# All of x0 as fp32 over hardware queues, part of the softmax on GpSimd, four exp transposes on TensorE, and a new order table in a fused attention and expert kernel

## The chip, the cores and the metric

The kernel runs on one core of a Trainium2 chip. A core has TensorE (PE, matrix products and transposes into PSUM), VectorE (DVE), ScalarE (ACT), GpSimd (POOL), SyncE (SP, which here only issues DMAs) and 16 DMA engines that all queues share. DMAs issued by SP and ACT go through hardware queues, those of POOL through a software queue, and only the latter convert a type on the way. The metric is the device time of one execution in microseconds, lower is better.

## The reference, cut to what matters

```python
B, H, S, Ns, D = (8, 8, 512, 32, 64)           # x: [B,H,S,D], state: [B,H,Ns,D], all fp32
scores  = softmax(scale * x @ state.T)         # over the 32 states   ("A side")
xread   = scores @ state                       # [B,H,512,64]
scores2 = softmax(scale * state @ x.T)         # over the 512 tokens  ("B side")
sread   = scores2 @ x                          # [B,H,32,64]
t = concat([xread, sread], axis=2) -> [N=4352, 512]
P = exp(t @ w_gate - max)                      # [N, 8]
for _ in range(8):                             # Sinkhorn
    P /= P.sum(1) + 1e-9;  P /= P.sum(0) + 1e-9;  P *= N / 8
out = sum over e of P[:, e] * (relu(t @ w1[e]) @ w2[e])    # w1 [8,512,1024], w2 [8,1024,512]
```

## The kernel before

All products run in fp16. The first part, up to some 134 us, is issued from a table (`PLAN`): every operation is made as an `Op` in program order and gets a number, and `issue` (L105) emits them in the order of the table. "63P" means operation 63 on PE; V is DVE, A is ACT, G is POOL, S is SP's DMA queue, H is bookkeeping of the program alone. Each engine runs its operations in that order and waits in it. The pairs of numbers at each `Op` (costs in us), ranks and due times served to make the table; nothing of them is computed on the chip. After the table, experts 1 to 7 run in plain loops (`layer1`, `layer2`, L263 to L387).

What the table holds, with the lines:

- **State.** Two DMAs of 256 KB (L441, SP and ACT) bring it as fp32; two copies each (L483) place it twice side by side as fp16; sixteen PE transposes (L492) and four evictions (L496) make stT, the state transposed. stD (L504 to L512) is a block form of it for the first two units.
- **x.** For each of the 8 batches two DMAs on POOL's queue (L468) bring x converted to fp16 into x_nat, which has four buffers, so that the load of batch 4 waits for the last reader of batch 0. Batches 0 and 1 are transposed by PE (L578) and evicted (L582), the others by transposing DMAs on SP (L591). The result is xT.
- **Units.** Half a batch (four heads) is a unit, u = 2b + q, 16 in all. A score product (L605) fills psB, of which there is one buffer: the next unit's score waits until this one's is read. A side: DVE turns the scores (L628, "flip"), takes maxima (L631), subtracts (L648), ACT takes exp (L656), DVE sums and takes reciprocals (L666, L667), DVE or POOL normalizes (L670), DVE turns back into aT (L674). Units 0 and 1 instead have a score product straight in token order (L684, then L688 and L691), and a transpose back by PE (L709) with an eviction (L712). B side: maximum (L640), bias (L644), exp with sum on ACT (L652), reciprocal (L659), normalization on DVE or POOL (L662), a transposing DMA on SP (L742) into ETs, a product with x (L758, "read") and an eviction into xsT.
- **Expert 0.** V = stT x w1 (L870), a hidden product of 512 tokens in eight blocks from V and aT (L897), relu on ACT or DVE (L425, L427), output product in halves (L935) and its eviction into acc (L419, L421). acc is first written here.
- **Gates and Sinkhorn.** Gate products (L788), the global maximum (L814 to L825), then eight rounds of row normalization (L829 to L833), a column sum by PE (L846) and column normalization (L839 to L841).
- **Towards expert 1.** Its weights, two V products, the hidden blocks of batch 0, and eight differences of weight halves, T (L965), all on DVE.

Weights come in four DMAs per expert on POOL's queue (L545, L548). An operation that writes PSUM or a buffer takes a slot of a ring and waits until the slot's last users are done.

Of the kernel before, what the change touches and what calls it, by code (L numbers as in the profile page):

```python
# [16 lines left out]
6G 0S 1S 2V 7H 44V 3A 33V 32A 34A 8G 56P 36P 35V 55H 37V 10H 45V 57A 42P 58V 9G 38P 40P 43A 59P 4S 39A 41V 5V  # L17
46V 62P 50H 51G 61A 71V 63P 60A 52G 64V 11G 72V 73A 80P 65V 12G 435P 401P 66A 81V 13H 79P 14G 82V 436A 88V
437A 404P 83A 67V 402A 137H 403A 89V 96H 97P 100P 84V 406A 68V 90A 98A 15G 85V 69P 86P 53G 405A 99V 87V 70A
103P 101A 102A 91V 409P 16H 92G 413P 104V 407P 410A 411P 105V 111A 438P 120P 414V 408A 419P 421P 106V 415P  # L20
112V 138S 121V 74V 439A 412A 422V 113V 417P 107A 54G 440A 75G 122V 432P 429P 123V 370V 420A 469P 128A 418A
416A 17G 108V 140P 124A 125V 423P 426P 471A 433P 114A 148V 93S 129V 430P 149V 172H 424P 76S 434A 115V 470A
109G 130V 139S 110V 126G 141V 131A 427P 18G 127V 142V 428V 431A 445P 143V 132V 94P 150A 95V 77P 425A 156P 116G
447P 151V 133V 78V 449P 446A 443P 441P 144A 455P 164V 152G 448A 117S 19H 450V 157V 444A 165V 173S 442A 451P
456A 166A 134S 20G 452A 453P 463P 158V 472P 207H 145V 175P 159V 183V 184V 457P 31G 146G 454A 176V 473A 160A
464P 185A 174S 460P 458P 461P 465A 147V 161V 21G 153S 177V 191P 47P 162G 474A 118P 167V 459A 154P 462A 178V
163V 135P 49A 168G 199V 22H 48V 179A 466P 136A 352P 475P 200V 192V 201A 193V 119V 467P 476A 194V 23G 195A 485P
202V 208S 210P 180V 169S 155A 218V 356P 353A 481P 357V 468A 487P 219V 24G 489P 181G 186V 211V 242H 486A 482A
477P 490V 488A 483P 479P 220A 170P 478A 503P 187G 480A 484V 171A 203G 196V 537P 209S 25H 212V 226P 197G 504A
505A 506P 213V 500P 182V 198V 26G 234V 221V 507A 222V 204S 188S 491P 27G 538A 227V 539A 501P 497P 502A 508A  # L30
492P 235V 243S 228V 244S 214A 229V 511P 215V 236A 523P 230A 498P 494P 216G 245P 495P 515P 512V 499A 277H 231V
524A 493A 517P 246V 253V 223S 496A 247V 521P 516A 237V 254V 519P 509P 522V 518A 248V 513P 232G 189P 520A 255A
205P 510V 224P 514V 540P 28H 278S 261P 249A 190V 269V 29G 225A 270V 262V 531P 534P 206V 238G 250V 532P 256V
358P 271A 535P 217V 541A 533A 233V 542A 312H 279S 263V 272V 536A 354P 280P 528P 543P 529P 525P 288V 289V 251G
555P 264V 281V 265A 282V 239S 257V 526P 359A 266V 544A 530V 556A 545P 355A 547P 549P 273G 553P 527A 546V 571P
313S 290A 548A 283V 605P 550A 554V 296P 267G 606V 304V 572A 305V 240P 573A 557P 284A 607A 558A 551P 297V 552A
568P 360P 258S 241V 285V 30G 291V 306A 559P 562P 574P 298V 252V 315P 299V 286V 569P 576A 268V 323V 563P 575A
274S 300A 560P 570A 292G 316V 361A 561A 581P 564A 307V 565P 362P 324V 317V 301V 325A 302G 566P 363V 582A 326V
579P 587P 583P 287V 314S 588V 591P 567A 580A 639P 608P 584A 592A 347H 303V 331P 577P 348G 641V 640A 610A 609A
339V 293S 589P 585P 275P 332V 259P 578A 327G 586A 260A 590A 294P 340V 308G 333V 341A 593P 309S 318V 319A 334V  # L40
295V 364P 594P 276V 328S 625P 619P 342V 595A 335A 365A 599P 320V 602P 343V 336V 600P 337V 603P 626A 321G 322V
329P 310P 350G 344S 601A 349G 311A 620V 345P 338V 346V 604V 366P 596P 330A 368P 369V 351G 597P 367A 371V 611P
372P 598A 695H 615P 617P 373V 612V 374P 375V 613P 614V 616A 623P 618A 621P 696H 711H 376A 705P 377V 642P 624A
622A 706A 707A 630P 643V 697V 708P 644A 378P 379V 631P 710A 627P 698V 380V 647P 632A 709A 636P 628P 381P 633P
699V 648V 637P 382V 634P 657P 629A 638A 383V 700V 653P 658A 655P 384P 651P 635A 701V 654A 725P 385V 723P 386V
702V 656A 726A 716P 652A 724A 717A 645P 659P 649P 714P 646A 650A 660A 387P 721P 715A 712P 727P 687P 722A 388V
728A 688A 667P 713A 664P 389V 390P 703V 665P 668P 391V 673P 674A 392V 661P 670P 669A 729V 393P 671P 394V 666A
662P 672A 677P 395V 718P 663A 678A 679P 675P 683P 719A 681P 720V 680A 676A 685P 396P 684A 682A 397V 686A 692P
704V 689P 693P 690P 730P 398V 694A 399P 733P 731V 691A 732A 735A 734A 400V
""".split()  # L50
ENGINES = {"P": "PE", "V": "DVE", "A": "ACT", "G": "POOL", "D": "DMA", "S": "SPQ", "H": "HOST"}
NT_ = 2
ETX = 0
POOLB = 1
# [50 lines left out]
def issue(ops):  # L105
    for step in PLAN:
        op = ops[int(step[:-1])]
        assert all(d.end for d in op.after) and ENGINES[step[-1]] in op.on
        for slot in op.takes:
            slot.ring.taken.append(slot)  # L110
            slot.tile = slot.make()
        op.emit(ENGINES[step[-1]])
        op.end = True
    assert all(op.end for op in ops) and len(PLAN) == len(ops)
# [3 lines left out]
def kernel(  # L118
# [99 lines left out]
    etp = actx.enter_context(tc.tile_pool(name="attn_et", bufs=3))  # L218
# [216 lines left out]
    st_in = spl.tile([128, B, NQ, 2, D], FP16, name="st_in")  # L435
    st_st = spl.tile([128, B, NQ, D], FP32, name="st_st")
    loads = []
    for g in range(2):
        def load(g=g):
            bs = ds(g * B // 2, B // 2)  # L440
            (nc.scalar if g else nc.sync).dma_start(  # L441
                out=st_st[:, bs], in_=state[bs].rearrange("b (q h) n d -> (h n) b q d", q=NQ))

        loads.append(dma((0, 0), 1.0, load, lands=2.7))
        ops[-1].since, ops[-1].hard = 0.5, 1
# [5 lines left out]
    wgd = dma((0, 2), 0.1, lambda: nc.sync.dma_start(  # L451
        out=wg_st, in_=moe_w_gate.rearrange("(kc p) e -> p kc e", p=128)))
    wgc = op((15.0,), {"DVE": (0.15, 0.25)}, lambda _: nc.vector.tensor_copy(out=wgh, in_=wg_st), [wgd])
    wgc.since = 20.0
# [7 lines left out]
    for b in range(B):  # L462
        x_ready.append([])
        part("x%d" % b)
        got = op((0, 1 + 2 * b), {"HOST": (0.0, 0.0)}, lambda _: None, takes=[xn[b]])
        for g in range(2):
            def load(b=b, g=g):
                nc.gpsimd.dma_start(  # L468
                    out=xn[b].tile[:, ds(g * 4, 4), :],
                    in_=x[b, ds(g * 4, 4), :, :].rearrange("h (p sc) d -> p h (sc d)", sc=NSC))  # L470

            x_ready[b].append(dma((0, 1 + 2 * b, g), 1.28 if b else 2.3 - 0.6 * g, load, [got], [], [xn[b]], "POOL"))
            ops[-1].since, ops[-1].hard = 0.7, 1
# [4 lines left out]
    bd = []  # L478
    for g in range(2):
        for s_ in range(2):  # L480
            def place(eng, g=g, s_=s_):
                bs = ds(g * B // 2, B // 2)
                copy(eng, st_in[:, bs, :, s_, :], st_st[:, bs])  # L483

            bd.append(op((0, 0, g), {"DVE": (0.50, 0.64)} if s_ else {"ACT": (0.50, 0.65)}, place, loads[g:g + 1] + warmed))
    stT_ready = []
    for g in range(4):
        ps = psum([128, 4, 128], FP16, "stT_ps")

        def turn(_, g=g, ps=ps):  # L490
            for i in range(4):
                nc.tensor.transpose(ps.tile[:, i], st_in[:, 2 * g + i // 2, i % 2].rearrange("p s d -> p (s d)"),  # L492
                                    identh)

        def keep(eng, g=g, ps=ps):
            copy(eng, stT[:, ds(2 * g, 2)].rearrange("p b q c -> p (b q) c"), ps.tile)  # L496

        t = op((0, 1, g), {"PE": (0.35, 0.55)}, turn, bd[g // 2 * 2:g // 2 * 2 + 2] + [makeh], [ps])
        stT_ready.append(op((0, 1, g), EVICT16, keep, [t], uses=[ps]))
    ND = (TOK + 1) // 2  # L500
    stD_ready = {}
    if TOK:
        stD = spl.tile([128, ND, NQ, 4, 2, Ns], FP16, name="stD")
        zd = op((0, 0, 0), {"POOL": (0.40, 0.50), "DVE": (0.25, 0.35)}, lambda eng: engines[eng].memset(stD, 0.0))  # L504
        for b in range(ND):
            def spread(eng, s_, b=b):
# [4 lines left out]
                               lambda eng, s_=s_, spread=spread: spread(eng, s_), stT_ready[b // 2:b // 2 + 1] + [zd])  # L511
# [55 lines left out]
    for b in range(B):  # L567
# [4 lines left out]
                  [x_ready[b][0]], [xT])  # L572
        for g in range(2 if b < NT else 0):
# [11 lines left out]
            t = op((due_x(2 * b + g) - 2.0, 0), {"PE": (0.70, 0.88)}, turnX, [x_ready[b][g], makeh], [ps], [xn[b]])  # L585
# [3 lines left out]
        for g in range(0 if b < NT else 2):  # L589
# [5 lines left out]
            xt_ready.append([dma((due_x(2 * b - 2), 0, g), 2.0, turn, [x_ready[b][g], gotT], [], [xn[b], xT], lands=0.8)])  # L595
            ops[-1].moves, ops[-1].xbar = (3.0, 0.8), 1
            ops[-1].on = {"SPQ": (1.4, 4.5)}
        for q in range(NQ):
# [18 lines left out]
            o2 = op((due_x(2 * b + q), 0), {"PE": (0.13, 0.38)}, score, xt_ready[q] + stT_ready,  # L617
# [5 lines left out]
            E2 = slot(etp, 3, [128, S], FP16, "E2")  # L623
            a16 = slot(asb, 2, [128, S // 32, Ns], FP16, "a16")
            ETs = slot(etp, 3, [128, NSC, 128], FP16, "ETs")
# [402 lines left out]
    n = 0  # L1028
# [79 lines left out]
```

## Time and profile before

| what | us |
|---|---|
| median of 3 runs (753.98 to 754.52) | 754.13 |
| the profiled execution, device time | 753.05 |
| its span, first to last instruction | 751.3 |
| first transpose of x on PE (L578) | 6.98 |
| first hidden product of expert 0 (L897) | 18.66 |
| first row normalization of Sinkhorn (L829) | 102.90 |
| last product of the table before expert 1's A (L334) | 134.45 |
| DVE busy in 20 to 100 us | 73.2 of 80 |

When the loads of the first 25 us were issued and how long they took shows in the DMA issues of the first 40 us: x_nat 5.9 us to landing in the median, w1h 8.7, w2h 10.4, the two state loads 4.9 and 4.3, the transposing DMAs 5.0 and 4.8. The profile lists busy time per engine, then waits with the one who ended them; the clock column of a stretch is the share of full speed that TensorE was granted.

### The profile page before, as it was taken

What the parts mean: (1) busy time and instruction counts of PE and PEld (TensorE: products, weight loads), DVE (VectorE), ACT (ScalarE), POOL (GpSimd) and SP (SyncE); (2) the same over time, 40 slices, a digit from 0 to 9 for tenths busy, and PEclk for the clock granted to TensorE, in tenths of its full rate; (3) what the DMA queues carried; (4) which work ended last, traced back from release to release, by engine and by line L of the source; (5) the groups of instructions that cost most, each with busy time, mean ns of one, the idle gap of its engine ahead of it and who ended that gap; (6) DMA issues with size and microseconds to landing.
All of it is one profiled execution on the core that took longest, in us unless ns stands there. A gap on an engine that the chain in (4) does not pass through costs nothing.

```text
span 751.3 us, 16144 instructions
## 1 busy us (share of the span) xinstructions
PE 734.7 (98%) x6517; PEld 501.2 (67%) x6517; DVE 616.3 (82%) x1529; ACT 518.2 (69%) x1014; POOL 70.8 (9%) x81
## 2 busy tenths in 40 slices
PE   4999999999999999999999999999999999999997
PEld 3444445667677777777777677776777777776776
DVE  5999989888888789788887888887897888878875
ACT  6876846798976766666666766667667666676662
POOL 3664310200010000100000000100001000000000
PEclk9999999999999999999999999999999999999999
DMA  9997560600032000600006000330006000002234
GB/s 175 151 133 127 86 92 1 113 2 1 1 66 48 2 1 2 113 1 1 2 4 110 2 1 1 58 56 1 1 2 112 2 1 2 1 29 101 98 113 141
DMA packets 51323, 36.71 MB, mean 49 GB/s; under 512 B 25392, under 2 KB 43824, under 8 KB 51248
## 3 DMA queue, kind: packets, MB, share of 16 engines
q0 software_dynamic: 22272, 20.97, 18.4%
q1 hardware_dynamic: 27744, 14.18, 7.7%
q8 instruction: 51, 0.84, 0.5%
q10 hardware_dynamic: 1232, 0.52, 0.3%
q14 instruction: 24, 0.20, 0.1%
HBM read 42.48 MB, written 8.91 MB: 68 GB/s over the span
## 4 chain that ended last, share of the span: by engine, by line
PE 91%; DVE 3%; DMA 2%; ACT 1%; POOL 1%; issue 0%; SPq 0%; POOLq 0%; ACTq 0%
PE hps L255 28%; PE Bseed L334 20%; PE A L334 14%; PE E L334 13%; PE yps L935 6%; PE v_ps L235 4%; PE hps L897 4%; DMA xT<-x_nat 2%; DMA x_nat<-in_x_dram 1%; DVE acc L348 1%; ACT Hm L275 1%; PE su_ps L758 0%; PE y L312 0%; PE v_ps L870 0%; POOL E L662 0%; ACT V L419 0%
## 5 line engine op out<-in xcount | busy, mean ns | idle before, releaser
L275 ACT ACTIVATE Hm<-hps 128x512 f16<-128x512 f32 (+1 forms) x496 | 265.2, 577 | 128.1 <-PE hps L255 125.3
L255 PE MATMUL hps<-aT,V 128*128 128x512 f16 x880 | 230.1, 379 | 0.0
L334 PEld LDWEIGHTS <-Hm 128*128 128x128 f16 x1888 | 181.4, 98 | 71.2 <-issue 15.8
L348 DVE SCALAR_TENSOR_TENSOR acc<-Bseed,Pmat,acc 128x256 f32<-128x256 f32 x354 | 155.0, 477 | 9.4 <-PE Bseed L334 6.6
L334 PEld LDWEIGHTS <-sm 128*128 128x128 f16 x1416 | 138.2, 98 | 34.1 <-issue 0.4
L334 PE MATMUL A<-w2h,Hm 128*128 128x256 f16 x944 | 123.7, 273 | 0.0
L334 PE MATMUL Bseed<-T,Hm 128*128 128x256 f16 x944 | 123.3, 273 | 0.0
L255 PEld LDWEIGHTS <-V 128*128 128x128 f16 x880 | 86.1, 98 | 51.3
L348 DVE SCALAR_TENSOR_TENSOR acc<-E,Pmat,acc 128x256 f32<-128x256 f32 x236 | 103.1, 476 | 12.5 <-PE E L334 12.5
L281 DVE TENSOR_TENSOR sm<-Hm 128x512 f16<-128x512 f16 (+1 forms) x122 | 50.1, 411 | 64.2 <-ACT Hm L275 64.0
L243 ACT CAST V<-v_ps 128x512 f16<-128x512 f32 x150 | 77.7, 611 | 0.0
L348 DVE SCALAR_TENSOR_TENSOR acc<-A,Pmat,acc 128x256 f32<-128x256 f32 x118 | 51.9, 479 | 17.2 <-PE A L334 16.7
L935 PE MATMUL yps<-w2h,hT 128*128 128x512 f16 x272 | 64.1, 379 | 0.0
L363 ACT COPY Bseed<-A 128x512 f32<-128x512 f32 (+1 forms) x62 | 34.1, 550 | 43.3 <-PE A L334 42.1
L334 PE MATMUL E<-T,sm 128*128 128x256 f16 x472 | 61.7, 273 | 0.0
L334 PE MATMUL E<-w2h,sm 128*128 128x256 f16 x472 | 61.7, 273 | 0.0
L334 PE MATMUL Bseed<-T,sm 128*128 128x256 f16 x472 | 61.5, 272 | 0.0
L282 DVE TENSOR_TENSOR Hm<-Hm 128x512 f16<-128x512 f16 (+1 forms) x122 | 50.2, 412 | 4.2
L284 DVE TENSOR_TENSOR sm<-Hm,sm 128x512 f16<-128x512 f16 (+1 forms) x122 | 50.2, 412 | 4.2
L283 DVE TENSOR_TENSOR sm<-sm,Hm 128x512 f16<-128x512 f16 (+1 forms) x122 | 49.4, 405 | 0.0
L194 POOL DMA_DIRECT2D w1h<-in_moe_w_dram x12 | 8.5, 714 | 397.9 <-PE hps L255 397.4
L935 PEld LDWEIGHTS <-hT 128*128 128x128 f16 x272 | 25.4, 99 | 28.8 <-issue 1.7
(127 smaller groups left out, 609.7 us busy)
## 6 DMA issues: line engine op xcount, KB each, us to landing
w1h<-in_moe_w_dram POOLq DMA_DIRECT2D x16, 512.0 KB, 7.0
w2h<-in_moe_w_dram POOLq DMA_DIRECT2D x16, 512.0 KB, 8.1
out_dram<-acc SPq DMA_DIRECT2D x32, 256.0 KB, 2.6
x_nat<-in_x_dram POOLq DMA_DIRECT2D x16, 256.0 KB, 5.6
st_st<-in_state_dram ACTq DMA_DIRECT2D x1, 256.0 KB, 4.9
st_st<-in_state_dram SPq DMA_DIRECT2D x1, 256.0 KB, 4.3
ETs<-E SPq DMA_TRANSPOSE x16, 3.9
out_dram<-acc SPq DMA_DIRECT2D x4, 64.0 KB, 1.7
```

The lines of the kernel that those rows point to most:

```text
L235: nc.tensor.matmul(ps[q][ds(j * Ns, Ns), :], stT[ds(r, 64), bi, q, ds((j ^ q) * Ns, Ns)], w1h[ds(r, 64), 2 * q + j // 2, cols], tile_posit ...
L243: nc.scalar.copy(out=dst, in_=src)
L255: nc.tensor.matmul(out, lhs, rhs, start=(k == 0), stop=(k == len(terms) - 1))
L275: nc.scalar.activation(out=Hm[:, i, j, :tn], in_=hps[:, :tn], func=AF.Relu)
L281: nc.vector.tensor_add(s1, a21, a22)
L282: nc.vector.tensor_sub(a21, a11, a21)
L283: nc.vector.tensor_sub(s2, s1, a11)
L284: nc.vector.tensor_sub(s4, a12, s2)
L334: nc.tensor.matmul(dst[:, c], lhs(j, c), rhs[:, j], start=first and c == 0 and j == 0, stop=(j == NJ - 1), skip_group_check=True)
L348: nc.vector.scalar_tensor_tensor(out=dst, in0=src[:, c], scalar=p[:, k], in1=dst, op0=ALU.mult, op1=ALU.add)
L363: nc.scalar.copy(out=Bb[:, :nk], in_=A[:, :nk])
L935: nc.tensor.matmul(yps.tile, hT[fb].tile[:, ds(tk * 128, 128)], w2h[:, fb, :], start=(fb == 0), stop=(fb == NFB - 1))
```

## The change

The order table is new as a whole, since operations were added and removed and so renumbered (736 before, 747 after; POOL has 67 entries instead of 50, SP 28 instead of 31). The parts:

- **x0** comes as fp32 in four hardware DMAs (two on SP, two on ACT) into a part of acc that is not yet in use, and four copies on DVE and ACT make fp16 of it. ACT's second one is issued after its exp table is loaded.
- **State** comes in rows of 1 KB per partition: a quarter by SP, ahead of x0, a quarter and a half by POOL's queue. One copy per quarter places it twice; evictions reorder the columns. Consumers wait for their own quarter, not for all four. The gate weights' load waits for the first eviction.
- **GpSimd** gets 12 of the 14 subtractions of the A side (units 2 to 10 and 13 to 15), and seven of the eight T differences. Its B normalizations (11 instead of 12) become a product with a broadcast reciprocal.
- **TensorE** transposes the exps of units 0 to 3 (ETX = 4) in place of SP's DMAs; E2 and ETs have four buffers instead of three.
- **Idle transposes**: `IDLE` puts 70 transposes or products without use ahead of nine operations of PE, written into the PSUM tile that the operation is about to fill: 32 ahead of the first state transpose, 18 ahead of the first V product, and 2 to 6 ahead of seven others.

```diff
-ETX = 0
+IDLE = {38: 32, 63: 2, 41: 3, 69: 2, 83: 6, 412: 18, 85: 2, 76: 3, 94: 2}
+ETX = 4
+XH = 2
+NE2 = 4
...
+        idle(op.takes[0].tile if op.takes else None, IDLE.get(int(step[:-1]), 0))
         op.emit(ENGINES[step[-1]])
...
+    st_in = spl.tile([128, B // 2, 4, 2, D], FP16, name="st_in")
+    st_st = spl.tile([128, B // 2, 4 * D], FP32, name="st_st")
+    st_rows = state.rearrange("b h (k l) d -> (b h k) (l d)", l=4).rearrange("(g p) c -> p g c", p=128)
+    xs = acc[:, ds(0, 2 * XH), :].rearrange("p (g t) d -> p g (t d)", t=2)
...
+    def load_st(a, b):
+        return begin("SPQ", lambda: nc.sync.dma_start(out=st_st[:, a:b], in_=st_rows[:, a:b]), 0.35 * (b - a))
+
+    def load_x(g, k):
+        q = nc.scalar if k else nc.sync
+        return begin("ACT" if k else "SPQ", lambda: q.dma_start(
+            out=xs[:, g, ds(k * 512, 512)].rearrange("p (h c) -> p h c", h=2),
+            in_=x[0, ds(4 * g + 2 * k, 2)].rearrange("h (p sc) d -> p h (sc d)", sc=NSC)), 0.68)
+
+    loads = load_st(0, 1)
+    xs_in = [[load_x(g, k) for k in range(2)] for g in range(XH)]
+    for a, b in ((1, 2), (2, B // 2)):
+        def load_rest(eng, a=a, b=b):
+            (nc.gpsimd if eng == "POOL" else nc.sync).dma_start(out=st_st[:, a:b], in_=st_rows[:, a:b])
...
+                def narrow(eng, g=g, k=0):
+                    copy(eng, xn[0].tile[:, ds(4 * g + 2 * k, 2), :].rearrange("p h c -> p (h c)"),
+                         xs[:, g, ds(k * 512, 512)])
...
+        def place(eng, g=g):
+            copy(eng, st_in[:, g], st_st[:, g].rearrange("p (l d) -> p l d", d=D).unsqueeze(2)
+                 .broadcast_to((128, 4, 2, D)))
...
-            copy(eng, stT[:, ds(2 * g, 2)].rearrange("p b q c -> p (b q) c"), ps.tile)
+            copy(eng, stT[:, ds(2 * g, 2)].rearrange("p b q (m l) -> p (b q m) l", l=4), ps.tile.rearrange("p (l m) -> p m l", l=4))
...
+    wgd = dma((0, 2), 0.1, lambda: nc.sync.dma_start(
+        out=wg_st, in_=moe_w_gate.rearrange("(kc p) e -> p kc e", p=128)), [stT_ready[0]])
...
-            o2 = op((due_x(2 * b + q), 0), {"PE": (0.13, 0.38)}, score, xt_ready[q] + stT_ready,
+            o2 = op((due_x(2 * b + q), 0), {"PE": (0.13, 0.38)}, score, xt_ready[q] + st_ready(b),
...
-            E2 = slot(etp, 3, [128, S], FP16, "E2")
+            E2 = slot(etp, NE2, [128, S], FP16, "E2")
...
             def normB(eng, E2=E2, rrec=rrec):
-                engines[eng].tensor_scalar(out=E2.tile, in0=E2.tile, scalar1=rrec.tile, scalar2=None,
-                                           op0=ALU.mult)
+                if eng == "POOL":
+                    nc.gpsimd.tensor_mul(E2.tile, E2.tile, rrec.tile.broadcast_to((128, S)))
+                else:
+                    nc.vector.tensor_scalar(out=E2.tile, in0=E2.tile, scalar1=rrec.tile, scalar2=None, op0=ALU.mult)
...
-                s1 = op(r(4), {"DVE": (0.60, 0.80)}, subA, [m1], [], [eA, mxA])
+                s1 = op(r(4), {"DVE": (0.60, 0.80), "POOL": (1.05, 1.20)}, subA, [m1], [], [eA, mxA])
...
-        nc.vector.tensor_sub(T[:, i, jj], p[:, jj], q[:, jj])
+        engines[eng].tensor_sub(T[:, i, jj], p[:, jj], q[:, jj])
...
+    def idle(t, n):
+        if not n:
+            return
+        t = t.rearrange({2: "p a -> p a", 3: "p a b -> p (a b)", 4: "p a b c -> p (a b c)"}[len(t.shape)])
+        for _ in range(n):
+            if t.dtype == FP16:
+                nc.tensor.transpose(t[:, :128], identh, identh)
+            else:
+                w = min(128, t.shape[1])
+                nc.tensor.matmul(t[:, :w], identh, identh[:, :w], start=True, stop=True, skip_group_check=True)
```

In the new table the operations that the prediction names stand as follows. PE up to the first hidden block: stT 0, xT00, stT 1, score 0 and its token form, stT 2, xT01, stT 3, xT10, token form of 1, score 1, xT11, the exp transpose of unit 0, V of batch 0 first half, read 0, A0's transpose, score 2, V second half, A1's transpose, V of batch 1 first half, score 3, the exp transpose of unit 1. DVE up to A1's eviction: st_place0, x0's first narrowing, stT 0, both halves of xT00, half of stD, st_place2, then the softmax of units 0 and 1 with all of xT01 and xT11 between. POOL: identity, state quarters, x1, weights w0 first two, normB 0, x2 first half, third weights, normB 1, x2 second half, the subtraction of unit 2, fourth weights, x3 first half, and so on: loads and arithmetic in one queue.

## The prediction

> **What bounds the kernel now.** I read the page first, then busy time in stretches, the waits of TensorE (PE), the chain of waits, and the groups of VectorE (DVE) and GpSimd (POOL). The page's engine line and the stretches (us; then for each engine busy time and count, the granted PE clock, DMA share, GB/s):
>
> ```profile
> PE 734.7 (98%) x6517; PEld 501.2 (67%) x6517; DVE 616.3 (82%) x1529; ACT 518.2 (69%) x1014; POOL 70.8 (9%) x81
> ```
> ```profile
> 0.00:5.00 5.00, 0.00 (x0) 0.00 (x0) 0.33 (x2) 1.49 (x2) 4.25 (x11) 1.00 0.69 128
> 5.00:10.00 5.00, 3.02 (x29) 3.02 (x30) 2.35 (x6) 2.81 (x5) 3.26 (x5) 1.00 1.29 181
> 10.00:15.00 5.00, 3.18 (x65) 1.60 (x63) 4.76 (x11) 3.83 (x9) 0.00 (x0) 1.00 1.32 198
> ...
> 50.00:60.00 10.00, 8.62 (x74) 3.56 (x68) 9.15 (x19) 7.76 (x17) 5.25 (x6) 1.00 0.93 145
> ...
> 70.00:80.00 10.00, 10.00 (x89) 4.65 (x88) 9.58 (x22) 7.74 (x18) 3.65 (x4) 1.00 0.51 80
> ```
>
> From 140 us on PE is busy without a break, and the diff leaves that part alone: a microsecond won or lost before the order table ends (134.45, the first A product of expert 1) is one at the end. Inside the table two engines matter: PE from about 19 us on, and DVE, over 9 tenths busy to about 90. The waits of PE:
>
> ```profile
> PE xT_ps L578 <- DMA x_nat<-in_x_dram: 8.1, 3, 7.0
> PE psB L605 <- DMA xT<-x_nat: 2.2, 3, 0.9
> ```
>
> So 7.0 us pass before the first x is there, and three scores wait for a transposing DMA. Then the clock; the first two lines are of the stretches, the others of the chain (start, us, what):
>
> ```profile
> 17.00:18.00 1.00, 0.96 (x8) 0.69 (x8) 0.91 (x2) 1.00 (x5) 0.00 (x0) 0.50 1.50 213
> ...
> 19.00:20.00 1.00, 1.00 (x4) 0.41 (x3) 0.97 (x2) 0.87 (x3) 1.00 (x1) 0.50 1.24 204
> ```
> ```profile
> 18.66 2.65 PE hps L897 x8
> ...
> 73.88 1.73 PE hps L897 x8
> ```
>
> The first hidden products of expert 0 start at 18.66 at half clock: eight take 2.65 us where they later take 1.73, a loss of 0.92. What the change moves between DVE and GpSimd (18.28 to 103 us for DVE, 0 to 137 for POOL; busy, mean ns, idle before):
>
> ```profile
> L648 DVE TENSOR_TENSOR eA<-eA,mxA 128x512 f32<-128x512 f32 x14 | 10.4, 748 | 0.1
> L427 DVE TENSOR_SCALAR hT<-hps 128x512 f16<-128x512 f32 x15 | 10.1, 678 | 1.8 <-PE hps L897 1.8
> L628 DVE STREAM_TRANSPOSE eA<-psB 128x512 f32<-128x512 f32 x14 | 9.9, 704 | 1.4 <-POOL a L670 1.4
> ```
> ```profile
> L662 POOL TENSOR_SCALAR E<-E,rrec 128x512 f16<-128x512 f16 x12 | 19.2, 1600 | 18.7 <-DVE rrec L659 14.4 <-ACT hT L425 4.0
> L670 POOL TENSOR_TENSOR a<-eA,rA 128x512 f16<-128x512 f32 x12 | 12.8, 1066 | 21.6 <-DVE rA L667 12.2 <-DVE logits L421 4.2 <-ACT logits L419 2.4
> ```
>
> DVE's subtraction L648 averages 748 ns where its neighbours take 680 to 700, and POOL idles 40 us ahead of its 24 operations: there is room for the move.
>
> **The head, to the first hidden product.** All orders below are counted off the two order tables. x0 now comes as fp32 on SP and ACT with the first quarter of the state (0.13 MB, then 1.05 MB). In the trace hardware loads start moving data at 1.9 us, though issued at 0.7, and move 215 GB/s from 1.9 to 3.8 (256-byte pieces); stores of 2 KB pieces at 744 to 746 reach 381. The 1 KB pieces of x0 are not shown and lie between. The first 0.66 MB then take 1.7 to 3.0 us, plus 0.75 to be known (the state's 0.5 MB should end at 4.3 by that rate, its first copy starts at 5.08): x0's first half at 4.4 to 5.7, I take 5.0. Narrowing adds a copy (L421 rows like it: 0.57 us) where before x landed at 6.93 ready. The other three quarters of the state now go by POOL's software queue: its first data are later than 3.8. Alone at its 199 GB/s (10 to 20 us) 0.39 MB land at 6.5; behind all that is left of x0, at 10.1; I take 8.1, the middle, as both run at once.
>
> That landing matters, since st_place2 stands in DVE's order ahead of the whole first softmax. From it to the eviction of A1 the new table has on DVE (row means): place 0.57, four row maxima 2.72, two biases 0.28, two subtractions 1.38, two sums with reciprocal 1.86, two norms 1.22, two reciprocals 0.28, four xT evictions 1.68, the flip of unit 2 0.70, wg cast 0.17, A1's eviction 0.42: 11.3. For the old order the same addition from 10.67 gives 8.30 and the trace took 8.03, a factor 0.97: 10.9. So 8.1 + 10.9 = 19.0 against 18.70, **0.3 later**. Bounds: 0.8 earlier (x0's own path of narrowing 0.6, transposes 0.6 to 1.0, evictions 0.8, spread and score 0.5 reaches DVE's maxima at 7.6), 2.3 later. The quicker x start is eaten by DVE work: both halves of xT01 and xT11 are evicted there now.
>
> TensorE's extras here are hidden: 70 idle transposes or products (32 of them by 4.9 us at the 0.107 us of a cold one, 16 in 1.71), two transposes of an exp with evictions, and the first read fill time in which PE waits for DVE; uncovered, the 38 later ones would cost 3.0 to 4.1 (0.078, eight in 0.62 at 14.84, to 0.107). They may hold the clock, worth at most the 0.92; as DVE sets the pace just after, I count only the 0.38 DVE then waited for hps, within the idle time below. By the Trainium skill (TensorE: Matmul & The Clock Gate, Part 1: The HAM clock gate) the clock halves after an idle window of some 3.4 us and returns after a busy one; the steps of this trace agree. With the clock held and PE in command the sum would be 0.5 lower.
>
> **From there to the Sinkhorn loop.** By DVE's order to the first row normalization (L829, 102.90): 12 subtractions go to POOL (12 x 0.75 = 9.0), one flip falls into the head (0.7), 2 reciprocals, 5 small evictions and a memset leave (1.5); 6 PSUM evictions of 0.68 (4.1), 3 of transposed exps (1.3), a normA (0.7), a normB and a gate eviction (0.5) come. Net 4.7, by 0.97 **4.5 us less**. POOL takes the subtractions at 1.07 each (L670's row, fp32 out not shown; 0.75, DVE's own, to 1.85, L296's fp32 row, are the bounds) and its 11 normBs become a tensor_mul; nearest is L670 again, 1.07 for 1.60. POOL was busy 5 of 10 us here, so it has room; uncovered, the chain of a unit grows by 0.3.
>
> But PE's table now has more behind the first column product (L846, 105.25): 6 hidden blocks (2.6), one output half (0.9), two V products (0.7): **4.1 more** (rounded down). PE alone could be there at 19.0 + 76.4 = 95.4 (50 hidden blocks of 0.43, 48 halves of 0.865, the rest from their rows), DVE at 105.25 + 0.3 - 4.5 = 101.05. DVE decides, so what counts is its idle time: 6.8 of the 80 us from 20 to 100. Gaps of 0.79, 1.19 and 0.20 hang on scores that wait for xT, and 0.38 on the cold clock. Four exps leave the SP queue, whose other transposes then come sooner: of these 2.6 I take **1.8 as gone** (bounds 0, 2.6). The Sinkhorn chain has 5 us more PE work beside it and hides.
>
> Other edits cost nothing: the gate weights' load waits for stT's first eviction; behind it on SP is only the transpose of x2, which waited to 17.4 for its load anyway. Last weights half w0: now behind a subtraction on POOL, issue 20.6 (was 20.49), landing 26.6, wanted at 26.6; uncovered, up to 1. Seven T1 sums on POOL (1.07 each) end by 115, wanted at 134. Four buffers of E2 and ETs free, not delay.
>
> **Sum.** +0.3 - 4.5 + 4.1 - 1.8 = -1.9. The profiled execution took 753.05 (span 751.3); it becomes 751.15. The median is 754.13, so I say **752.2**; own range 750.3 (both gains whole: 0.8 early, 2.6 gone: -3.8) to 754.6 (2.3 late).
>
> **Rivals.**
> Slower: POOL's queue starves the scores. x loads now stand behind subtractions: x3's second half behind A3's norm, x5's behind A6's and A7's subtractions, and on SP x5's transposes in turned order behind B7's. Before, x5's second load was issued at 44.90 and the score waited at 60.10; now I get 44.3, and a score that PE's own work would allow at 52.5 but xT at 54 to 57. PE's waits are free up to 5.6 us (101.05 - 95.4); past that point each counts. With 8 in all (4 here, 4 at x3, x6, x7) the first column product comes at 103.4, and with 33.3 of work behind it (29.2 before) the table ends at 136.7, 2.2 later: **756.3**. For it: transposes took 5.0 to 6.3 beside loads. Against: 3.1 in quiet, and four fewer.
> No change: DVE keeps all its idle time, and 4.5 is returned as 4.1: -0.1, **754.0**. For it: each unit waits on a chain over four engines.
> Interlock: a DVE subtraction at 41.32 took 1.17 instead of 0.68, its first 0.6 beside a POOL operation. In the Sinkhorn loop the seven POOL sums meet some five two-input DVE steps; at 0.5 to 1.07 each 2.5 to 5.4, less the chain's 2.4 of slack: about +1.5 on the forecast, **753.7**. The Trainium skill (SBUF — State Buffer, Who interferes with whom) says so: two SBUF inputs on DVE and a reading GpSimd exclude each other. That also speaks for taking 12 such steps off DVE.
> More: head early and idle gone, **750.3**.
>
> **Chances.** Forecast 0.31, slower 0.28, no change 0.15, interlock 0.12, more 0.14. Runs differ by 0.5 us, so 0.2% (1.5 us, 752.6 to 755.6) is what can be told: faster 0.45, within 0.27 (the middle two), slower 0.28. Range 749.9 to 756.4: it takes in the slower case's price, leaving its worse half and the best tail out.
>
> **What would show it.** First xT transpose near 5.7 (was 6.98); st_place2 near 8.1; first hps at 19 and eight in 1.73; L648 twice after it on DVE and 12 times on POOL at 1.07; first column product at 99.3; PE's waits at psB under 5.6. Wrong if st rows land after 9, if a score waits over 4 us, or if DVE idles over 7 us from 20 to 100.

## The result and the profile after

The changed kernel takes 757.85 us in the median of 8 runs (754.79 to 758.45), the kernel before 754.07 in 8 runs beside it: a ratio of 1.0044, interval 1.003 to 1.0058. It is slower, where 752.2 was forecast, and lies above the range of 749.9 to 756.4. The profiled execution took 758.45 us, its span is 756.7 (before 751.3).

The engine line of the page of the changed kernel, then its busy time in stretches (columns as for the kernel before):

```profile
PE 741.6 (98%) x6603; PEld 506.4 (67%) x6603; DVE 618.9 (82%) x1527; ACT 513.2 (68%) x1007; POOL 82.3 (11%) x98
```
```profile
0.00:5.00 5.00, 3.65 (x35) 3.65 (x36) 0.90 (x4) 2.10 (x3) 4.24 (x11) 1.00 0.64 183
5.00:10.00 5.00, 3.91 (x61) 2.90 (x59) 4.10 (x11) 3.29 (x7) 0.90 (x2) 1.00 1.31 249
10.00:15.00 5.00, 4.56 (x90) 3.56 (x88) 4.93 (x12) 5.00 (x12) 2.55 (x3) 1.00 1.24 206
...
30.00:35.00 5.00, 1.70 (x12) 0.69 (x13) 1.33 (x4) 0.61 (x2) 0.45 (x1) 0.85 1.49 108
...
50.00:60.00 10.00, 10.00 (x107) 4.48 (x105) 9.74 (x21) 7.81 (x19) 5.92 (x7) 1.00 0.89 127
70.00:80.00 10.00, 10.00 (x54) 4.34 (x52) 9.68 (x21) 7.58 (x17) 4.23 (x5) 1.00 0.94 131
```

The stretch to read is 30 to 35. All four engines mostly stand still in it (PE busy 1.70 of 5 us, DVE 1.33, ACT 0.61, POOL 0.45) while the DMA engines are at least as busy as at 5 to 15 and move half as much (108 GB/s where it was 249 and 206). From 50 to 90 PE is full and DVE busy 97 to 99% (92 to 96% in the kernel before). So up to there the loss has one place. The waits of PE (us in total, times, longest) name it, and the chain of waits (start, us, what) shows where it comes from:

```profile
PE psB L636 <- DMA xT<-x_nat: 4.2, 1, 4.2
PE csb_ps L879 <- DVE cpart L866: 1.7, 3, 0.8
```
```profile
15.77 0.99 POOL E L694
16.75 5.96 DMA x_nat<-in_x_dram
...
22.73 10.52 DMA xT<-x_nat
...
33.30 0.30 PE psB L636 x8
33.60 1.82 PE yps L968 x4
35.42 1.70 PE hps L930 x4
```

POOL normalizes unit 1, only then issues the second load of x2 (16.75), and the transposing DMA that follows takes 10.52 us. The score of unit 5 starts at 33.30. The products behind it are cold: 1.82 us for four that take 0.86 at full clock. In the kernel before, the same transposing DMA was issued later and took 4.5 us (timeline of SP, then the time to landing of that one DMA):

```profile
25.96 1.32 SPq L591 DMA_TRANSPOSE xT<-x_nat  x1
DMA to landing us min/median/max: 4.5/4.5/4.5
```

The head went as forecast, or a little better. x0's first half was there at 5.61 and the first transpose of x ran at 6.21 (6.98 before; both some 0.5 later than forecast), but the late state rows, which decide, landed at 7.83, and the first hidden products started at 18.50 at full clock, twelve in 2.8 us where before eight took 2.65:

```profile
L930 PE MATMUL hps<-aT,V 128*128 128x512 f16 x12 | 2.8, 379 | 0.0
```

What moved between the engines did so at the forecast prices. The groups of POOL are its 12 subtractions, its row normalizations of the A side and its product with a broadcast reciprocal (1600 ns each before, as a product with a scalar):

```profile
L679 POOL TENSOR_TENSOR eA<-eA,mxA 128x512 f32<-128x512 f32 x12 | 12.5, 1045 | 12.0 <-DVE mxA L662 10.8 <-ACT E L683 1.1
L703 POOL TENSOR_TENSOR a<-eA,rA 128x512 f16<-128x512 f32 x11 | 11.8, 1072 | 6.0 <-DVE rA L700 4.0 <-ACT hT L430 1.3 <-ACT V L424 0.3
L694 POOL TENSOR_TENSOR E<-E,rrec 128x512 f16<-128x512 f16 x11 | 11.4, 1037 | 23.6 <-DVE rrec L690 21.1 <-ACT E L683 1.8 <-ACT hT L430 0.8
```

The second loss is in the Sinkhorn loop. Its timeline (start, us) in the second round, DVE and then POOL:

```profile
106.77 0.77 DVE L863 TENSOR_SCALAR rsum<-rsum 128x34 f32<-128x34 f32 x1
107.57 0.37 DVE L864 RECIPROCAL rsum<-rsum 128x34 f32<-128x34 f32 x1
107.97 0.94 DVE L865 TENSOR_TENSOR Pmat<-Pmat,rsum 128x272 f32<-128x272 f32 x1
```
```profile
106.35 1.15 POOL L998 TENSOR_TENSOR T<-w2h,T 128x512 f16<-128x512 f16 x1 [3.53 <-DMA w2h<-in_moe_w_dram]
107.46 2.47 POOL L998 TENSOR_TENSOR T<-w2h 128x512 f16<-128x512 f16 x2
```

The two DVE steps that lie beside POOL's sums take 0.77 and 0.94 us, in the rounds without sums 0.18 and 0.44; the reciprocal between them keeps its 0.37. The three column products that wait for these rounds are PE's 1.7 us.

The whole difference to the forecast is in three stretches of the profiled execution:

| stretch | forecast | measured | off by |
|---|---|---|---|
| first column product | 99.3 | 104.47 | 5.2 |
| from there to expert 1's first A product | 33.3 | 34.75 | 1.45 |
| from there to the end (before: 616.85) | 616.85 | 617.48 | 0.6 |

These add to 7.3, and 751.3 - 1.9 + 7.3 is the span of 756.7.

### The profile page after: what moved, and what is told of

Read it like the earlier page. It is cut to its first block, busy times and chain, and to the rows that moved or that the text cites. A ratio compares the mean times of both kernels' runs of the same rounds, so it can differ in the third digit from the quotient of the medians.

```text
span 756.7 us, 16312 instructions
## 1 busy us (share of the span) xinstructions
PE 741.6 (98%) x6603; PEld 506.4 (67%) x6603; DVE 618.9 (82%) x1527; ACT 513.2 (68%) x1007; POOL 82.3 (11%) x98
## 4 chain that ended last, share of the span: by engine, by line
PE 88%; DVE 6%; DMA 3%; ACT 1%; issue 0%; POOL 0%; DVEq 0%; POOLq 0%; ACTq 0%
PE hps L260 27%; PE Bseed L339 20%; PE A L339 14%; PE E L339 13%; PE yps L968 5%; PE v_ps L240 4%; PE hps L930 3%; DMA xT<-x_nat 1%; DMA x_nat<-in_x_dram 1%; DMA st_st<-in_state_dram 1%; DVE acc L353 1%; ACT Hm L280 1%; PE y L317 0%; DVE nmB L671 0%; DVE hT L432 0%
## 5 line engine op out<-in xcount | busy, mean ns | idle before, releaser
L353 DVE SCALAR_TENSOR_TENSOR acc<-A,Pmat,acc 128x256 f32<-128x256 f32 x118 | 51.9, 479 | 17.2 <-PE A L339 16.7
L968 PEld LDWEIGHTS <-hT 128*128 128x128 f16 x272 | 25.4, 98 | 30.4 <-issue 2.9
```

The source lines that it names most:

```text
L353: nc.vector.scalar_tensor_tensor(out=dst, in0=src[:, c], scalar=p[:, k], in1=dst, op0=ALU.mult, op1=ALU.add)
L968: nc.tensor.matmul(yps.tile, hT[fb].tile[:, ds(tk * 128, 128)], w2h[:, fb, :], start=(fb == 0), stop=(fb == NFB - 1))
```

## The experiments

Edits of the table are given as the order of the entries on the engine that they touch; 19G and 20G are the two loads of x2, 58G to 61G the four of expert 0's weights, 22G and 23G those of x3, 25G and 26G of x4, 82G, 100G and 125G normalizations of units 0 to 2, 115G, 133G and 154G subtractions of units 2 to 4. On each chip the kernel before ran beside these: medians 753.60, 753.65 and 753.62 us of 17 to 26 runs.

### Where does the wait of 4.2 us come from?

**x2's loads ahead of the normalizations.** Both are issued at 5.9 and 6.6 instead of 12.1 and 16.75.

```diff
-POOL: 59G 82G 19G 60G 100G 20G 115G 61G 22G
+POOL: 59G 19G 20G 82G 60G 100G 115G 61G 22G
```

> Theory A (late load): score 5 waits 4.2 us at 33.30 because x2's second load stands on POOL's queue behind the B normalization of unit 1 (issued 16.75, its transpose at 22.73). With both x2 loads ahead of the B normalization of unit 0 the load lands by 20 and the transpose by 26: no wait at score 5, no half clock at 33 to 37, 754.1 minus 1 to 2. Theory B (crowding): the transposing DMA is slow because software loads run beside it whatever its issue time; then it lands 8 to 10 us after its issue here too, and the total falls by at most 2 from 757.85. Theory C (Sinkhorn interlock alone costs the time): nothing changes, 757 to 758.

Measured: 754.39 us (753.86 to 756.79), ratio 1.0013 [1.0001, 1.0025]. The transposing DMA of x2's second half, now issued at 19.2, took 7.4 us; the score of unit 5 came at 30.4 and waited for nothing. DVE was busy 73.8 of the 80 us from 20 to 100 (69.4 in the changed kernel) and the first column product came at 99.82. So the place of x2's two loads in POOL's queue is worth 3.5 us between the medians (757.85 and 754.39), and with it mended the forecast's 99.3 is missed by 0.5 only. PE is busy 80.27 of the 80.65 us from its first hidden product (19.17) to the column product, DVE 74.42: the profile, which models where products end, shows PE idle for 0.4 us only. PE's two largest waits from the first hidden product up to expert 1 are then these (the same list as above), and behind them 0.3 at expert 1's entry:

```profile
PE csb_ps L879 <- ACT V L424: 0.8, 1, 0.8
PE csb_ps L879 <- DVE cpart L866: 0.7, 1, 0.7
```

**x4's first load later**, out of the 10.5 us of that transposing DMA:

```diff
-POOL: 22G 133G 25G 118G 125G 136G 23G
+POOL: 22G 133G 118G 125G 136G 23G 25G
```

> x4's first load (issued 22.91, beside the transpose of x2's second half) is put behind x3's second load; x2's own load stays late. Theory A: the wait at score 5 stays, 4 us, 757 to 758. Theory B: the transpose lands 6 us after its issue instead of 10.5, score 5 waits below 1, and the kernel gains 3 to 5: 753 to 755.

Measured: 755.29 us, ratio 1.0039 [1.0019, 1.006], in two groups: six runs at 754.04 to 755.34, four at 758.12 to 759.74. The profiled one is of the first: the DMA took 7.1 us, scores 5 and 6 waited 0.6 each:

```profile
30.07 0.30 PE L636 MATMUL psB<-xT,stT 64*32 64x256 f16 x8 [0.58 <-DMA xT<-x_nat]
```

x2's own load was as late here as in the changed kernel (issued at 16.88 for 16.75), and the first column product still came at 99.88. So in this execution the lateness of the load cost at most 0.6 us of waiting; the rest of the 4.2 is the length of the transposing DMA. Since four runs stay slow, the load of x4 is part of what makes it long, but not the whole.

**x4's first load sooner**, ahead of the subtraction before it and so of the transposing DMA:

```diff
-POOL: 22G 133G 25G
+POOL: 22G 25G 133G
```

> x4's first load stands right behind x3's first, so it is issued near 21.7, ahead of the transpose of x2's second half (22.4 to 23.7) and not within its issue. Theory of overlapping issue: the transpose lands in 6 to 8 us as in the good runs, none or few of the runs above 756.5. Theory of crowding by bytes: the same bytes stand in front of it or more, it lands 10 us after its issue or later in as many runs as in the changed kernel (6 of 8) or more, 757 to 759.

Measured: 757.7 us (754.58 to 758.83, again two groups), ratio 1.0041 [1.0024, 1.0058]; no better than the changed kernel. The transposing DMA, issued at 24.6 with three loads under way, took 8.8 us, and score 5 waited 3.15 at 33.4. That speaks for how much is under way at once, not for one load issued at the same moment.

Over the thirteen traces, count the loads of POOL's queue that are under way when one of the first transposing DMAs (issued before 32) starts, or begin within 1.05 us of it: with at most two, 25 cases took 4.5 to 7.9 us; with three or four, 13 cases took 5.8 to 12.6, eight of them 9.9 or more. This, and the limit of 1.05 us with it, was chosen after the traces were seen. In the changed kernel's profiled run there were three (two under way, x4's 0.2 us later), in a run of the version with the sums on DVE, below, two (x4's 1.2 us later), 10.5 and 7.5 us. Why the same program gives now one, now the other was not settled; the changed kernel's own runs lie at 754.79 and 755.67, and six at 757.39 to 758.45.

**Is it the cold clock behind the wait?** 60 idle transposes ahead of score 5:

```diff
-IDLE = {38: 32, 63: 2, 41: 3, 69: 2, 83: 6, 412: 18, 85: 2, 76: 3, 94: 2}
+IDLE = {38: 32, 63: 2, 41: 3, 69: 2, 83: 6, 412: 18, 85: 2, 76: 3, 94: 2, 167: 60}
```

> Sixty idle products ahead of score 5 keep PE busy while it waits. Clock theory: half speed at 33.5 to 36.9 cost 1.8 us of PE (four output products 1.82 instead of 0.86, four hidden ones 1.70 instead of 0.86); it goes away and the kernel gains up to 1.8: about 756. Rival: DVE sets the pace there and PE's lost time is slack: below 0.5. An idle fp32-bank product may also lengthen the wait where the transpose lands early.

Measured: 757.64 us (756.4 to 759.36), ratio 1.0061 [1.004, 1.0082]. The clock stayed whole, the first column product still came at 105.39 and the table ended at 140.15. By the medians, 0.2 apart with four runs spread over 3 us, the half clock behind the wait is not what the kernel loses. The trace can't say why: its execution was the longest of the four and waited for a transposing DMA three times (0.9, 1.2, and 1.7 at 58.7), 3.8 us in all.

### The sums on POOL

**All eight T differences on DVE**, as before the change:

```diff
-708G 709G 710G 711G 712G 713G 714V 715G
+708V 709V 710V 711V 712V 713V 714V 715V
```

> The seven T differences go back to DVE, in the same places. Interlock theory: the row steps L863 and L865 go back from 0.8 and 0.94 us to 0.2 and 0.44, the three waits for the column product (1.7 us in all) fall below 0.6, and the kernel gains 1 to 1.7: near 756.5. Rival: DVE has seven more operations of 0.41 in the Sinkhorn loop, 2.9 us, and the chain is as late as before or later: 757.5 to 759.

Measured: 756.53 us (752.98 to 758.38), ratio 1.0052 [1.0035, 1.007]; five runs, spread over 5.4 us, most likely by the transposing DMA; the median lies where it was expected, but that alone tells little. The profiled run (752.98) had the short one and shows the loop by itself (timeline of DVE, start and us, third round):

```profile
107.02 0.18 DVE L863 TENSOR_SCALAR rsum<-rsum 128x34 f32<-128x34 f32 x1
...
107.64 0.44 DVE L865 TENSOR_TENSOR Pmat<-Pmat,rsum 128x272 f32<-128x272 f32 x1
```

The steps are back at 0.18 and 0.44, the eight sums cost 0.42 each on DVE (1.15 to 1.43 on POOL), and PE's waits for column products fall from 1.7 to 0.3 us: 100.03 to 133.76 is 33.7, where 34.75 was: 1.0 less, although DVE has more to do. The Trainium skill (SBUF — State Buffer, Who interferes with whom) states that DVE's scalar operations in its 2-port modes, like its operations with two SBUF inputs, can't run beside a GpSimd instruction that reads, while a reduction can. The trace agrees: 0.18 to 0.77, 0.44 to 0.94, and the row sum L862 at 0.42 to 0.44 throughout; which mode L863 ran in no run shows.

**Both edits**, x2's loads early and the sums on DVE.

> Both edits: x2's loads early and the T differences on DVE. The two losses are at different places, so they should add: 754.4 of the early loads less the 1.2 to 1.8 of the interlock, 752.6 to 753.2, no run above 756; the forecast of 752.2 would then have missed these two alone. Rival: one of the two hides the other, and it stays at 754.

Measured: 753.12 us (752.51 to 755.83), ratio 0.9996 [0.9985, 1.0007]: no difference from the kernel before that can be told. The first column product came at 100.29, expert 1's first A at 134.03. The two losses are separate and add up: 3.5 and 1.3 us by the medians of the single edits, 4.7 for both.

### Single parts of the change

**The subtractions back on DVE**, on top of x2's early loads:

```diff
-115G 133G 154G 170G 189G 205G 224G 240G 259G 310G 329G 345G
+115V 133V 154V 170V 189V 205V 224V 240V 259V 310V 329V 345V
```

> On top of the early x2 loads the 12 subtractions go back to DVE. DVE theory (DVE sets the pace up to the Sinkhorn loop): 12 x 0.7 = 8.4 us more on DVE, of which some 2 to 4 fit in its idle time: the first column product comes near 104 to 106 instead of 99.8 and the kernel takes 758 to 761. Rival (the chain over the engines or PE sets it): 754 to 755.5, as with the early loads alone.

Measured: 760.44 us (759.92 to 761.11), ratio 1.0087 [1.0071, 1.0104], 6.0 us above the same kernel with them on POOL. DVE is busy 76.2 of the 80 us (73.8), the first column product comes at 105.89. Not all of it is DVE's work: without the subtractions POOL issued the last weights load and x3 three microseconds sooner (17.2 and 18.0), the two transposing DMAs took 10.1 and 12.6 us, and 1.5 us of PE's waits are that. The rest wait for DVE or for what it feeds:

```profile
PE psB L636 <- DMA xT<-x_nat: 1.5, 1, 1.5
PE v_ps L903 <- DVE hT L432: 1.2, 1, 1.2
...
PE hps L930 <- DVE xsT L426: 0.8, 1, 0.8
```

**The subtractions alone on POOL, in the kernel before.** Nothing else of the change; the order on every engine as it was.

```diff
-s1 = op(r(4), {"DVE": (0.60, 0.80)}, subA, [m1], [], [eA, mxA])
+s1 = op(r(4), {"DVE": (0.60, 0.80), "POOL": (1.05, 1.20)}, subA, [m1], [], [eA, mxA])
...
-106V 123V 143V 159V 178V 194V 213V 229V 248V 299V 318V 334V
+106G 123G 143G 159G 178G 194G 213G 229G 248G 299G 318G 334G
```

> The kernel before, with one part of the change alone: the subtractions of units 2 to 10 and 13 to 15 on GpSimd, everything else, and the order on every other engine, as it was. My prediction counted 9.0 us off DVE for it. Theory 1, DVE sets the pace up to the first column product (105.25): DVE's busy time in 20 to 100 falls from 73 to some 66, and the column product comes sooner, but no more than TensorE's own idle time allows with its order unchanged (2.25 us in 20 to 100, 0.9 of cold clock before it): 104 to 104.8, time 752.5 to 753.7. Theory 2, the subtraction delays the loads and normalizations behind it in POOL's queue: waits for x or for a normalization grow, the column product at 106 to 108, time 754.5 to 757.

Measured: 759.48 us (758.05 to 760.85), ratio 1.0076 [1.0061, 1.009]; worse than either expectation. DVE's busy time did fall, from 73.2 to 62.7, and the first column product came at 110.65 instead of 105.25. The chain of waits at the largest wait of PE, 3.1 us:

```profile
31.63 0.04 POOL eA L648
...
32.67 1.57 POOL E L662
...
34.25 3.35 DMA ETs<-E
...
37.70 0.78 ACT E L652 x2
...
40.51 0.30 PE psB L605 x8
```

From 31.63 POOL subtracts for one unit (1.04 in its timeline), then normalizes another with the 1.57 us form, then SP's transposing DMA empties a buffer of E, of which there are three; ACT's exp waits for it, everything behind that exp in ACT's queue waits too, and PE gets its score at 40.51. The changed kernel has each of these links shorter: a normalization of 1.04, exps transposed by PE, four buffers. So the share of POOL costs 5.9 us without the other parts and saves up to 6.0 with them; the parts can't be priced one by one and added.

**No idle transposes**, on top of x2's early loads:

```diff
-IDLE = {38: 32, 63: 2, 41: 3, 69: 2, 83: 6, 412: 18, 85: 2, 76: 3, 94: 2}
+IDLE = {}
```

> The early x2 loads, and none of the 70 idle transposes and products. Clock theory: TensorE starts cold, the transposes of the head take 0.107 us each, the first hidden product comes 0.5 to 1 later and again at half speed: 755 to 755.5. Slack theory: DVE sets the pace from 8 us on, and the end is unchanged within 0.4: 754 to 754.8.

Measured: 756.18 us (754.66 to 757.0), ratio 1.0034 [1.0023, 1.0045], 1.8 above the same kernel with them and more than either expectation. Its stretches (PEclk is the third number from the end):

```profile
16.00:18.00 2.00, 1.24 (x20) 0.35 (x18) 1.97 (x5) 1.33 (x5) 1.03 (x1) 0.50 1.40 201
18.00:20.00 2.00, 1.56 (x23) 0.80 (x24) 1.99 (x5) 1.26 (x3) 0.00 (x0) 0.50 1.24 207
```

The clock is at half from 15.5 to 22.3, the first hidden products start at 20.16 instead of 19.17, at half clock in both runs, and the first column product comes at 102.31 instead of 99.82. With the idle transposes the profiled runs had 3.4 us of half clock (x2 early) or none (the changed kernel, up to 33).

### A version below both kernels

**V for expert 1 earlier**, on top of both edits: the first V product of the second weight half and its two evictions ahead of the last output products.

```diff
-PE:  700P 703P 701P 704P 410P 741P 744P
+PE:  741P 700P 703P 701P 704P 410P 744P
-ACT: 697A 702A 705A 742A 743A 745A
+ACT: 697A 742A 743A 702A 705A 745A
```

> The version with x2's loads early and the T sums back on DVE, and in addition the first V product of expert 1's second weight half with its two evictions on ACT moved ahead of the last output products of the table. In that version the table ended 0.42 us sooner than before's (134.03 against 134.45), but what follows it took 617.5 us instead of 616.85, and TensorE waited 0.27 us there for ACT's eviction of V. If that late eviction is the reason: span 751.5 - 0.6 = 750.9, time 0.3 to 0.6 below that version's 753.1, so 752.6, and no wait for V at the loop's entry. If the 0.6 us have another reason (the order of the relus of batch 8, say): 753.1 unchanged.

Measured: 752.92 us (752.66 to 753.86), ratio 0.9989 [0.998, 0.9997]. The wait for V at the entry is gone, and from expert 1's first A to the end it takes 617.2 instead of 617.5: half of the 0.6. Against the version without this edit the time tells nothing for sure; against the kernel before it is 0.7 us lower, with an interval that leaves 1 out, and it is the lowest of all.

**And the last weights load ahead of the first subtraction:**

```diff
-POOL: 60G 100G 115G 61G 22G
+POOL: 60G 100G 61G 115G 22G
```

> As the version before it, and the last of the four loads of expert 0's weights ahead of the first subtraction in POOL's queue. With x2 early and the sums on DVE, TensorE still waited 0.8 us for that load at 27.5 and 1.0 for a transposing DMA at 35.2. If a load's place in POOL's queue is what those waits hang on: the first is gone, the table ends 0.5 to 0.8 sooner, time 751.9 to 752.4. If the loads crowd each other whatever their order: another wait of like size for a transposing DMA or a load takes its place, 752.6 to 753.2.

Measured: 756.6 us (756.17 to 757.17), ratio 1.0036 [1.0024, 1.0048], 3.7 worse, more than either expectation. The wait for the weights is gone and two others stand in its place; the chain:

```profile
17.78 9.89 DMA xT<-x_nat
...
27.71 0.30 PE psB L636 x8
...
31.09 7.12 DMA xT<-x_nat
...
38.25 0.30 PE psB L636 x8
```

The load, 3.3 us earlier (16.8 for 20.1), makes the transposing DMAs of x2 take 9.9 and 12.0 us, where the version without this edit had 6.4 and 7.9. This is the controlled case of the count above: one load more under way, and nothing else changed.

## Why the prediction was wrong

**The step that failed** is the idle time of DVE: "of these 2.6 I take **1.8 as gone** (bounds 0, 2.6)", because four exps leave SP's queue and its "other transposes then come sooner". The second one of x2 did come sooner, at 22.73 instead of 25.96. What the prediction left out is that its length could grow: 10.52 us for 4.5, beside three loads of POOL's queue, so that it landed at 33.26 where the new order of PE wanted it at 29.1. That its load stood behind a normalization (16.75) put it where it can meet those loads; the lateness by itself cost at most 0.6 where the DMA took 7.1 us. DVE idled 10.6 of the 80 us instead of 6.8 before and 5.0 as forecast: 5.6 off, which with the head 0.5 early is, to 0.1, the 5.2 by which the first column product was late. With only x2's loads moved, DVE idled 6.2 and the product came at 99.82. Two of the prediction's signs of being wrong were there: a score that waited over 4 us, and DVE idle for over 7.

**The rival that came true, in part.** "POOL's queue starves the scores" had the mechanism, but sought it at x3, x5 and later; the one wait was at x2, whose second half the prediction had not followed. Its price was wrong too: "PE's waits are free up to 5.6 us". One wait of 4.2 us cost all of itself (104.47 against 99.82). The 5.6 came from 76.4 us of PE work up to the column product; at full clock throughout (x4's load later) the profile, which models where products end, counts 79.75 busy of 81.26 us, so that some 1.5 were free, and DVE waited for the same score. Which of the two engines sets the pace behind the wait was not separated: PE is full there, and yet 12 subtractions more on DVE cost 6.0 us.

**The interlock** was held a rival of its own, on the forecast +1.5. It came on top of the other: 34.75 us behind the first column product for 33.3, of which 1.0 is gone with the sums on DVE; by the medians it is worth 1.3 (754.39 and 753.12). So the mechanism was right and the size nearly; that the two exclude each other, as the chances had it, was not. Of the steps that were stretched, L863 has one tensor input, where the prediction counted those with two.

**What held.** The head (19.0 forecast, 18.50, with the state rows at 7.83 for 8.1). The subtractions and normalizations on POOL (1.07 for 1.045 and 1.037). The exchange of 4.5 us of DVE for 4.1 of PE work behind the first column product: 33.3 forecast there, 33.7 measured with the sums on DVE.

**What was mis-sized.** The idle transposes: 0.38 counted, 1.8 measured by taking them away. The prediction had "DVE sets the pace just after". Hidden products at half clock also come later to DVE and ACT, which evict them; whether the 1.8 arise in this way was not tested. The sums on POOL took 1.15 to 1.43 us each, where 1.07 was counted. And the end: nothing was counted for expert 1's entry, which cost 0.6; half of it went with V's earlier evictions, the cause of the rest is open.

**What stays open.** Why one and the same program takes now the long, now the short transposing DMA: the count of loads under way goes with it, and one load put earlier brought the long one, but only one execution of each kernel was traced. Other sizes of x2's and x3's loads, and the exps of units 2 and 3 back on SP, were not tried.

## What to carry to other kernels

Before an engine that issues loads is given arithmetic, walk its queue entry by entry, give each load a due time from what its consumer's engine waits for, and see which other transfers it will meet: here the meeting cost more than the lateness. Check a claimed slack against the busy time of a trace; where two engines are both nearly full, a wait of one is not free. And try parts together: here the same 12 subtractions on POOL cost 5.9 us in the old order and save up to 6.0 in the new one.

## What the hardware showed that was not expected

A transposing DMA of the same 256 KB took 3.1 to 4.1 us with no load of POOL's queue under way and, when issued before 32 us beside such loads, 4.5 to 12.6, and one load issued 3.3 us sooner changed two of them by 3.5 and 4.1 us. So "earlier" is not safe for a load either.

A DVE product with a scalar that has one SBUF input stalls beside POOL as well, more than the two-input ones that the prediction counted. The timeline of the changed kernel, DVE and then POOL:

```profile
44.61 1.25 DVE L696 TENSOR_SCALAR E<-E,rrec 128x512 f16<-128x512 f16 x1
```
```profile
44.64 1.06 POOL L679 TENSOR_TENSOR eA<-eA,mxA 128x512 f32<-128x512 f32 x1
```

It takes 0.31 to 0.35 us where POOL computes nothing (at 55.07 and 88.35), and 1.25 here. Three of DVE's five normalizations were stretched so, by 1.7 us in all (1.25, 0.88 and 0.63 against 0.35).

The clock was halved without an idle stretch of PE. In the kernel before it was at half from 16.83 to 20.24 us, and PE was busy 2.0 of the 3.4 us ahead of that; in the version with both edits PE was busy 2.1 us from 15.33 to 18.75 and the clock stayed whole. So where the prediction says that the steps of the trace agree with an idle window, only the length of the step, 3.4 us, does.
